# Linear attention with memory, and a Fourier mixing layer: a fourth part buffer, W8 in borrowed buffers, value weights loaded one per step, two chunks loaded earlier

## The chip, the core and the metric

The kernel runs on one core of a Trainium2 chip. The metric is the device time of one execution in microseconds. Before the change, three runs took 1090.06, 1090.17 and 1091.95 us, a median of 1090.17 us.

## The reference

Two independent results stand side by side in the output. The first is attention with a compressive memory over a sequence of 2048 positions, 576 channels and 32 heads of 18, cut into four segments of 512:

```python
q, k, v = x @ wq, x @ wk, x @ wv            # split into heads and 4 segments
for s in range(4):
    p = softmax(qs @ ks.T * scale + mask)   # causal inside the segment
    a_dot = p @ vs
    num, den = phi(qs) @ M, phi(qs) @ z + 1e-6   # phi(t) = t + 1 if t > 0 else exp(t)
    outs.append(g * num / den + (1 - g) * a_dot) # g = sigmoid(beta)
    M, z = M + phi(ks).T @ vs, z + phi(ks).sum()
a = concat(outs) @ wo
```

The second is a Fourier mixing layer with dense matrices on another input of the same shape:

```python
ar, ai = x @ dft_hid_re.T, x @ dft_hid_im.T
y = dft_seq_re @ ar - dft_seq_im @ ai
```

The output is `a` and `y` next to each other, 2048 by 1152.

## The kernel before

Every product is carried out on pairs of a high and a low part, so that the result keeps the precision of 32-bit floats: `split` (lines 53 to 55) lets ScalarE (ACT) copy the rounded high part and VectorE (DVE) subtract it from the raw values. The channel dimension, 576, is five row blocks of 128, where the fifth holds the last 64 channels twice, once for the high and once for the low part of the other operand.

The program has two stages. The first (lines 402 to 445) is the projection stage. It runs through the four segments. In each segment TensorE (PE) first opens the four query column blocks of the segment together (`open_qk`, line 196). Then `project_qk(s, m)` (line 208) finishes them and computes block 8, which holds the last 64 columns of both queries and keys (its weight is W8), and the key blocks 4 to 7. In segment 0 the order is 0 to 8. For each of the nine blocks, ACT and DVE cut the product, which stands in one of four rotating accumulators in PSUM, into three bfloat16 parts: ACT writes the first part into the part buffer `p` (line 219), DVE subtracts (`r`, line 220, which is the last reader of the accumulator in segment 0 and for keys), one step later ACT writes the second part (line 227) and GpSimd (POOL) the third (line 228), and one more step later a store sends `p` to `qd` or `kd` in device memory. Below, p(n) is the part buffer of the n-th block in the order of its segment, counted from 0, or the block m itself where the order is that of m, as in segment 0; in segments 1 to 3 the text names p(6) and p(7) by their key blocks 6 and 7. In segments 1 to 3 the query blocks also go through `phi` (line 172). Then, for each of four row blocks j, `project_v` (line 245) makes the values in two halves (`v`), `lookup` (line 303) reads the memory (`look`, `nd`, `am`, whose store to `amd` follows one step later), `k_natural` (line 237) transposes the keys back (`kt`, `knl`), and `accumulate` (line 278) adds to the memory on PE (line 286).

Deferred work goes through a clock of steps: `later(n, fn)` puts a call n steps ahead and `tick` (line 84) carries out what is due, so that the order on each engine is written out by hand. All loads and stores are issued by one queue, SyncE (SP), in program order; an instruction there that waits holds everything behind it.

The weights are loaded at the start. `load_w` (line 124) takes a buffer `raw` (five of them, `raw8` with four for W8) and issues the load at once; only the split waits for a step (lines 147 to 150). So the loads of the key weight, of W8 and of the value weight WV all stand on SP ahead of the first store. A warm-up of 32 small products (line 191) runs on PE before the first inputs have arrived. The part buffer `p` has three copies (line 217), `am` two (line 325).

In segment 3 the second stage is prepared: the Fourier weights are split (`h_split`, line 336), and the chunks of the other input are loaded (`c_load`, line 345, three buffers `craw`) and cut (`c_cut`, line 352). Chunks 0 to 2 are loaded there and chunks 0 and 1 cut on DVE; from then on `chunk(n)` (line 486) loads chunk n + 3 and cuts chunk n + 2 on POOL.

The second stage mixes the attention of 32 groups of heads with the Fourier products in one order on PE, which is fixed when the program is written (lines 749 to 756): `dense` gives its next product whenever its share of the estimated time is behind. The output projection closes the kernel.

Of the kernel before, what the change touches and what calls it, by code (L numbers as in the profile page):

```python
# [12 lines left out]
F32 = mybir.dt.float32  # L13
F32R = mybir.dt.float32r
F16 = mybir.dt.float16
BF16 = mybir.dt.bfloat16
# [6 lines left out]
S, D, H, DH, NSEG, L = 2048, 576, 32, 18, 4, 512  # L23
P = 128
# [12 lines left out]
def infini_attention_and_fnet(ctx: ExitStack, tc: tile.TileContext, xT, wqk, w8, wv, wo, beta, xtT, cT, hT, out):  # L37
    nc = tc.nc
    act, dve, pool, pe = nc.scalar, nc.vector, nc.gpsimd, nc.tensor
    dma = nc.sync.dma_start  # L40
# [12 lines left out]
    def split(hi, lo, raw, lo_engine=None):  # L53
        act.activation(hi, raw, AF.Copy)  # L54
        (lo_engine or dve).tensor_tensor(lo, raw, hi.bitcast(F32), OP.subtract)  # L55
# [25 lines left out]
    def later(n, fn, *a):  # L81
        due.setdefault(clock[0] + n, []).append((fn, a))
# [31 lines left out]
    def split_wk(w, k, raw):  # L114
        if k < 4:
            split(w[0][k], w[1][k], raw)
        else:
            t1, t2 = w[2], w[3]
            act.activation(t1, raw, AF.Copy)
            act.activation(t2, raw, AF.Copy)  # L120
            dve.tensor_tensor(t1[:64], raw[:64], t1[:64].bitcast(F32), OP.subtract)
            dve.tensor_tensor(t2[64:], raw[64:], t2[64:].bitcast(F32), OP.subtract)

    def load_w(src, cols, k, tag="raw"):
        raw = sb.tile([P, cols], F32, name=tag, tag=tag, bufs=5 if tag == "raw" else 4)
        dma(raw, src[k])
        return raw

    def weight(mk):
        return [[mk() for _ in range(4)] for _ in range(2)] + [mk() for _ in range(2)]  # L130

    def wide_tile(cols):
        return lambda: wide.tile([P, cols], F32R, name="wide", tag="wide")
# [9 lines left out]
        split_x(0, k)  # L143
        split_wk(WQ, k, raw)
    dma(g, bass.AP(tensor=beta.tensor, offset=beta.offset, ap=[[0, P], [1, H]]))
    WK, W8, WV = weight(wide_tile(L)), weight(lambda: sb.tile([P, P], F32R, name="w8", bufs=10)), weight(wide_tile(D))
    for w, src, cols, tag, when in ((WK, wqk[:, :, L:], L, "raw", (1, 1, 1, 1, 2)), (W8, w8, P, "raw8", (3, 3, 3, 4, 4)),
                                    (WV, wv, D, "raw", (5, 5, 6, 6, 7))):
        for k in range(5):
            later(when[k], split_wk, w, k, load_w(src, cols, k, tag))  # L150
    later(5, gates)

    pq_hi = sb.tile([P, 5, L], F32R, name="pq_hi")
# [36 lines left out]

    def warm_up():
        o = ps.tile([P, 1024], F32, name="kt", bufs=1)
        for _ in range(32):
            pe.matmul(o[:, :P], ident16, ident16, start=True, stop=True)

    def open_qk(s):
# [11 lines left out]
    def project_qk(s, m):  # L208
        if m in FIRST:
            o = FIRST.pop(m)  # L210
        else:
            o = ps.tile([P, L], F32, name="qk", tag="acc", bufs=4)
            chain(o, qk_terms(s, m))
        if m >= 4 and s < 3:
            KF[m] = sk.tile([P, L], F32, name="kf", bufs=5)
            act.activation(KF[m], o, AF.Copy)
        p = sb.tile([P, 3, L], BF16, name="p", bufs=3)
        r = sb.tile([P, L], F32, name="r", bufs=2)
        act.activation(p[:, 0], o, AF.Copy)
        dve.tensor_tensor(r, o, p[:, 0], OP.subtract)  # L220
        if s and (m < 4 or m == 8):
            n = P if m < 4 else 64
            c = m if m < 4 else 4
            phi(sb, "q", o[:n], n, pq_hi[:n, c], pq_lo[:n, c])

        def rest():
            act.activation(p[:, 1], r, AF.Copy)
            pool.tensor_tensor(p[:, 2], r, p[:, 1], OP.subtract)
            if m < 8:
                later(1, dma, (qd if m < 4 else kd)[s][(m % 4) * P:(m % 4 + 1) * P], p)  # L230
            else:
                later(1, dma, qd[s][4 * P:], p[:64])
                later(1, dma, kd[s][4 * P:], p[64:])

        later(1, rest)
# [67 lines left out]
    def lookup(s, j):  # L303
        js = slice(j * P, (j + 1) * P)
        nd = sb.tile([P, H, 19], F32, name="nd", bufs=2)
        o = []
        for c0, c1 in ((0, 3), (3, 5)):
            o.append(ps.tile([P, 3, 8, 19], F32, name="look", tag="acc", bufs=4))
            for c in range(c0, c1):
                for n, (a, m) in enumerate(((pq_hi, md_lo), (pq_hi, md_hi), (pq_lo, md_hi))):  # L310
                    pe.matmul(o[-1][:, c - c0], a[:, c, js], m[:, c], start=c == c0 and n == 0, stop=True,  # L311
                              skip_group_check=True)
            if c0 == 0:
                act.activation(nd[:, :21].rearrange("p (c h) e -> p c h e", c=3), o[0][:, :, :7], AF.Copy)
                yield
        act.activation(nd[:, 21:28], o[1][:, 0, :7], AF.Copy)
        act.activation(nd[:, 28:], o[1][:, 1, 4:], AF.Copy)
        dve.tensor_tensor(nd[:, 7:22:7], nd[:, 7:22:7], o[0][:, :, 7], OP.add)
        dve.tensor_tensor(nd[:, 28], nd[:, 28], o[1][:, 0, 7], OP.add)
        w = sb.tile([P, H, 1], F32, name="w", bufs=2)  # L320
        den = o[1][:, 2].rearrange("p h e -> p (h e)")[:, :H, None]
        dve.tensor_scalar(den, nd[:, :, DH:], 1e-6, None, op0=OP.add)
        dve.reciprocal(den, den)
        dve.tensor_tensor(w, den, g[:, :, None], OP.mult)
        am = sb.tile([P, H, DH], F32, name="am", bufs=2)
        pool.tensor_tensor(am, nd[:, :, :DH], w.to_broadcast([P, H, DH]), OP.mult)
        later(1, dma, amd[4 * s + j], am.rearrange("p h d -> p (h d)"))
        yield
# [7 lines left out]
    def h_split(ri, k):  # L336
        if k == 0:
            HW[ri] = weight(wide_tile(D))
        split_wk(HW[ri], k, HRAW.pop((ri, k)))

    c_raw, c_split = {}, {}
    CHUNKS = [c for ri in range(2) for c in
              [(xtT, tt, 5) for tt in range(NT)] + [(cT, (ri, tt, q), 4) for tt in range(NT) for q in range(4)]]

    def c_load(n):
        if n < len(CHUNKS):
            src, at, k = CHUNKS[n]
            t = sr.tile([P, 5, P], F32, name="craw", bufs=3)
            dma(t[:, :k], src[at])
            c_raw[n] = t  # L350

    def c_cut(n, engine=pool):
        if n < len(CHUNKS):
            raw = c_raw.pop(n)
            hi = sr.tile([P, 4, P], F32R, name="chi", bufs=3)
            lo = sr.tile([P, 4, P], F32R, name="clo", bufs=3)
            split(hi, lo, raw[:, :4], engine)
            t = None
            if CHUNKS[n][2] == 5:
                t = sr.tile([P, P], F32R, name="xtail", bufs=3)  # L360
                act.activation(t, raw[:, 4], AF.Copy)
                engine.tensor_tensor(t[64:], raw[64:, 4], t[64:].bitcast(F32), OP.subtract)
            c_split[n] = hi, lo, t
# [38 lines left out]
    for s in range(NSEG):  # L402
        more = s < 3
        if s == 0:
            warm_up()
        open_qk(s)
        if s:
            memory()
        else:
            tick()  # L410
        for n, m in enumerate((0, 1, 2, 3, 8, 4, 5, 6, 7) if s else range(9)):
            project_qk(s, m)
            tick()
            if not more and n >= 5:
                h_split(0, n - 5)
            if s in (1, 2) and n >= 4:
                load_x(s + 1, n - 4)
            if not more and n == 0:
                for k in range(5):
                    h_load(0, k)  # L420
            if not more and n == 4:
                p1k.close()
                sr = ctx.enter_context(tc.tile_pool(name="sb2r", bufs=1, side="right", reuse_waits="tile"))
                attention_tiles()
            if not more and n in (5, 6):
                stacks(sr, n - 5)
            if not more and n == 7:
                stack_load(0, 99)
                c_load(0)
        for j in range(4):  # L430
            if not more and j < 2:
                c_load(1 + j)
            project_v(s, j, lookup(s, j) if s else iter(()))
            if more:
                k_natural(j)
            tick()
            for k in ((0, 1), (2, 3), (4,), ())[j] if s == 0 else ():
                load_x(1, k)
            if more and j in (1, 2):
                split_x(s + 1, j - 1)  # L440
            if not more and j < 3:
                h_split(0, 4) if j == 0 else c_cut(j - 1, dve)
            if more and j:
                accumulate(j - 1)
    p1.close()
# [345 lines left out]
def _tail_twice(a):  # L791
    return np.concatenate([a, a[512:]], axis=0).reshape(5, P, a.shape[1])
# [26 lines left out]
```

## Time and profile before

| | us |
|---|---|
| median of three runs | 1090.17 |
| lowest and highest run | 1090.06, 1091.95 |
| the profiled execution | 1088.57 |
| its span in the profile | 1086.7 |
| segment 0 of the projections (start to the next `open_qk`) | 64.0 |
| segment 1 | 62.5 |
| segment 2 | 64.0 |
| segment 3 (to the first product of the second stage) | 60.4 |

The span is the time between the first and the last instruction that the profile shows; the execution's own time has 1.9 us around it. Times in the profile count from the start of the span. In its rows, "PE" is a product, "PEld" the loading of its stationary operand; an output and an input stand as `out<-in`, with the program's names. A row's bracket gives the idle time of the engine just before and what ended it.

### The profile page before, as it was taken

The numbers are of one execution on the slowest core, as the hardware profiler recorded it, in microseconds if no ns is written. First come the engines' busy times: TensorE is split into PE (matmuls) and PEld (weight loads), VectorE is DVE, ScalarE is ACT, GpSimd is POOL, SyncE is SP. The second block draws the span as 40 slices with busy tenths as digits, with TensorE's granted clock in tenths as the row PEclk, the third lists the DMA queues.
The fourth block names the chain that finished last, engine by engine and source line by source line (L and its number), as shares of the span: only waits on it lengthen the run. The fifth ranks groups of instructions, "written<-read, shape, count | busy, mean of one in ns | idle before, by whom it ended". The sixth has DMA issues, their size and how long they took to land.

```text
span 1086.7 us, 26387 instructions
## 1 busy us (share of the span) xinstructions
PE 1058.9 (97%) x9900; PEld 980.8 (90%) x9900; DVE 764.6 (70%) x1973; ACT 665.9 (61%) x1477; POOL 618.2 (57%) x716
## 2 busy tenths in 40 slices
PE   9898999989999999999999999999999999999998
PEld 7787989878999999999898999999999998999998
DVE  5544546565687877778888777887887888885343
ACT  5756566544576666666766666766666666666233
POOL 2455564644566666666575666656666666667000
PEclk9999999989999999999999999999999999999999
DMA  6425243356344454445443454335354455523474
GB/s 195 177 101 174 103 135 128 140 172 196 104 102 108 111 127 118 105 124 140 132 121 103 124 127 119 109 103 138 111 142 145 112 151 147 164 90 109 127 207 142
DMA packets 118480, 143.50 MB, mean 132 GB/s; under 512 B 45040, under 2 KB 77680, under 8 KB 118352
## 3 DMA queue, kind: packets, MB, share of 16 engines
q1 hardware_dynamic: 118352, 141.81, 45.1%
q8 instruction: 78, 1.28, 0.5%
q14 instruction: 50, 0.41, 0.1%
HBM read 102.32 MB, written 39.45 MB: 130 GB/s over the span
## 4 chain that ended last, share of the span: by engine, by line
PE 81%; DVE 7%; ACT 5%; DMA 3%; issue 2%; POOL 1%; SPq 1%; DVEq 0%; POOLq 0%; ACTq 0%
PE d L459 35%; PE s L618 6%; PE d L77 5%; PE v L77 4%; PE pv L686 4%; PE d L500 3%; PE d L501 3%; PE d L502 3%; PE t L653 3%; PE qk L204 3%; PE pv L687 2%; PE t L656 2%; PE m L286 2%; PE look L311 1%; PE qk L77 1%
## 5 line engine op out<-in xcount | busy, mean ns | idle before, releaser
L621 DVE CUSTOM_DVE_ANT_0 s<-s,causal 128x512 f32<-128x512 f32 (+3 forms) x512 | 249.6, 499 | 46.8 <-PE s L618 40.4
L55 POOL TENSOR_TENSOR clo<-craw,chi 128x512 fp32r<-128x512 f32 x158 | 209.9, 1328 | 113.8 <-ACT chi L54 92.2
L664 ACT ACTIVATE pf<-t 128x384 f32<-128x384 f32 (+1 forms) x384 | 203.1, 529 | 112.1 <-PE t L653 112.1
L459 PE MATMUL d<-wide,chi 128*128 128x288 f32 x1408 | 267.5, 307 | 0.0
L459 PEld LDWEIGHTS d<-wide,chi 128*128 128x128 f32 x1408 | 211.7, 189 | 5.0 <-issue 1.6
L459 PE MATMUL d<-wide,clo 128*128 128x288 f32 x704 | 181.3, 324 | 0.0
L663 ACT ACTIVATE phi<-t 128x384 f16<-128x384 f32 x256 | 124.9, 488 | 80.6 <-PE t L660 80.5
L675 DVE TENSOR_TENSOR plo<-pf,phi 128x512 f16<-128x512 f32 x128 | 136.1, 1063 | 31.3 <-ACT phi L672 30.5
L673 POOL TENSOR_TENSOR plo<-pf,phi 128x384 f16<-128x384 f32 x128 | 134.8, 1053 | 40.2 <-ACT pf L664 24.3
L618 PE MATMUL s<-ks,qs 108*128 108x512 bf16 (+3 forms) x512 | 131.9, 298 | 5.7 <-DVE negm L621 5.6
L459 PE MATMUL d<-ab,chi 128*128 128x288 f32 x640 | 127.1, 308 | 0.0
L459 PEld LDWEIGHTS d<-wide,clo 128*128 128x128 f32 x704 | 118.6, 189 | 5.1 <-issue 1.7
L667 POOL TENSOR_SCALAR_AFFINE_SELECT pf<-pf 128x512 f32<-128x512 f32 x128 | 86.4, 675 | 55.6 <-ACT pf L664 49.0
L54 ACT ACTIVATE chi<-craw 128x512 fp32r<-128x512 f32 x160 | 101.9, 637 | 16.3 <-DMA craw<-cT 6.8
L686 PE MATMUL pv<-vst,phi 128*128 128x55 bf16 x1280 | 104.0, 190 | 0.4 <-DVE og L706 0.3
L459 PEld LDWEIGHTS d<-ab,chi 128*128 128x128 f32 x640 | 98.3, 189 | 1.2
L687 PE MATMUL pv<-vst,plo 128*128 128x37 bf16 x1280 | 98.8, 180 | 0.0
L674 DVE TENSOR_TENSOR plo<-pf,phi 128x384 f16<-128x384 f32 x128 | 93.5, 731 | 2.0 <-ACT pf L664 2.0
L686 PEld LDWEIGHTS <-phi 128*128 128x128 f16 x1280 | 76.1, 96 | 19.0 <-DVE og L706 1.3
L459 PE MATMUL d<-ab,clo 128*128 128x288 f32 x320 | 85.5, 316 | 0.0
L500 PE MATMUL d<-wide,chi 128*128 128x288 f32 x256 | 85.1, 332 | 0.0
L672 ACT ACTIVATE phi<-pf 128x512 f16<-128x512 f32 x128 | 80.8, 632 | 0.9 <-POOL pf L667 0.7
(182 smaller groups left out, 2439.2 us busy)
## 6 DMA issues: line engine op xcount, KB each, us to landing
craw<-cT SPq DMA_DIRECT2D x128, 256.0 KB
qs<-qd SPq DMA_DIRECT2D x192, 72.0 KB
ks<-kd SPq DMA_DIRECT2D x192, 72.0 KB
craw<-xtT SPq DMA_DIRECT2D x32, 320.0 KB
out<-y SPq DMA_DIRECT2D x31, 288.0 KB
vd<-vs SPq DMA_DIRECT2D x16, 440.0 KB
vst<-vd SPq DMA_DIRECT2D x32, 220.0 KB
qd<-p SPq DMA_DIRECT2D x16, 384.0 KB
```

The lines of the kernel that those rows point to most:

```text
L55: (lo_engine or dve).tensor_tensor(lo, raw, hi.bitcast(F32), OP.subtract)
L77: pe.matmul(o, a, b, start=n == 0, stop=n == len(terms) - 1)
L459: pe.matmul(o[h], a, b[:, h * 288:h * 288 + 288], start=start, stop=stop)
L500: pe.matmul(o, xh[:, k], wl[k][:, cs], start=k == 0, stop=False)
L618: pe.matmul(o[:, c:c + w], q[:, i * P:w], k[:, :w], start=True, stop=True)
L621: dve.tensor_tensor_reduce(o[:, c:c + w], o[:, c:c + w], CAUSAL[0][:, L - w:], scale=-1.0, scalar=-LOWEST, op0=OP.add, op1=OP.min, accum_o ...
L663: act.activation(hi[:, r:r + w], o[:, :w], AF.Exp, bias=LIFT, scale=SCALE)
L664: act.activation(f[:, r:r + w], o[:, :w], AF.Exp, bias=LIFT, scale=SCALE)
L673: pool.tensor_tensor(lo[:, 896:], f[:, 896:], hi[:, 896:], OP.subtract)
L675: dve.tensor_tensor(lo[:, :512], f[:, :512], hi[:, :512], OP.subtract)
L686: pe.matmul(o, hi[:, c:c + P], v, start=j == 0, stop=False)
L687: pe.matmul(o[:, 18:], lo[:, c:c + P], v[:, 18:], start=False, stop=j == i)
```

## The change

- The part buffer `p` has four copies, `am` one.
- W8 is stored with the five row blocks side by side, so that it comes in two loads (four blocks of 128 columns together, and the fifth) instead of five. They land in the two `qe` buffers, which `phi` uses from segment 1 on. Four row blocks are split by one operation of 512 columns each on ACT and DVE, at step 4.
- The value weights are no longer loaded ahead: block k is loaded at step 3 + k and split three steps later, in steps 6 to 10 instead of 5 to 7.
- The warm-up has 44 products instead of 32.
- In segment 3, chunks 3 and 4 are loaded right after chunks 0 and 1 have been cut, and `c_load` skips them later.

```diff
-    WK, W8, WV = weight(wide_tile(L)), weight(lambda: sb.tile([P, P], F32R, name="w8", bufs=10)), weight(wide_tile(D))
-    for w, src, cols, tag, when in ((WK, wqk[:, :, L:], L, "raw", (1, 1, 1, 1, 2)), (W8, w8, P, "raw8", (3, 3, 3, 4, 4)),
-                                    (WV, wv, D, "raw", (5, 5, 6, 6, 7))):
-        for k in range(5):
-            later(when[k], split_wk, w, k, load_w(src, cols, k, tag))
+    WK, WV = weight(wide_tile(L)), weight(wide_tile(D))
+    for k in range(5):
+        later((1, 1, 1, 1, 2)[k], split_wk, WK, k, load_w(wqk[:, :, L:], L, k))
+    w8_hi, w8_lo = (sb.tile([P, 4, P], F32R, name=f"w8{n}") for n in "hl")
+    W8 = [[w[:, k] for k in range(4)] for w in (w8_hi, w8_lo)] + [sb.tile([P, P], F32R, name=f"w8t{n}") for n in "ab"]
+    raw8 = [sb.tile([P, L], F32, name="qe", bufs=2) for _ in range(2)]
+    dma(raw8[0], w8[:, :L])
+    dma(raw8[1][:, :P], w8[:, L:])
+
+    def split_w8():
+        split(w8_hi, w8_lo, raw8[0].rearrange("p (k c) -> p k c", k=4))
+        split_wk(W8, 4, raw8[1][:, :P])
+
+    later(4, split_w8)
+
+    def load_wv(k):
+        later(3, split_wk, WV, k, load_w(wv, D, k))
+
+    for k in range(5):
+        later(3 + k, load_wv, k)
...
-        for _ in range(32):
+        for _ in range(44):
...
-        p = sb.tile([P, 3, L], BF16, name="p", bufs=3)
+        p = sb.tile([P, 3, L], BF16, name="p", bufs=4)
...
-        am = sb.tile([P, H, DH], F32, name="am", bufs=2)
+        am = sb.tile([P, H, DH], F32, name="am", bufs=1)
...
-        if n < len(CHUNKS):
+        if n < len(CHUNKS) and n not in c_seen:
+            c_seen.add(n)
...
                 h_split(0, 4) if j == 0 else c_cut(j - 1, dve)
+            if not more and j in (1, 2):
+                c_load(2 + j)
```

More of the change, by code (lines that the diff above doesn't have):

```diff
@@ L122, in split_wk, with load_w @@
             dve.tensor_tensor(t2[64:], raw[64:], t2[64:].bitcast(F32), OP.subtract)
-    def load_w(src, cols, k, tag="raw"):
-        raw = sb.tile([P, cols], F32, name=tag, tag=tag, bufs=5 if tag == "raw" else 4)
+    def load_w(src, cols, k):
+        raw = sb.tile([P, cols], F32, name="raw", tag="raw", bufs=5)
         dma(raw, src[k])
@@ L339, in h_split @@
         split_wk(HW[ri], k, HRAW.pop((ri, k)))
-    c_raw, c_split = {}, {}
+    c_raw, c_split, c_seen = {}, {}, set()
     CHUNKS = [c for ri in range(2) for c in
@@ L800 @@
         "wqk": _tail_twice(np.concatenate([wq[:, :512], wk[:, :512]], axis=1)),
-        "w8": _tail_twice(np.concatenate([wq[:, 512:], wk[:, 512:]], axis=1)),
+        "w8": _tail_twice(np.concatenate([wq[:, 512:], wk[:, 512:]], axis=1)).transpose(1, 0, 2).reshape(P, 5 * P),
         "wv": _tail_twice(wv),
```

## The prediction

> **What bounds the kernel now.** I read the page first, then the windows by stage, the waits, the chain of waits, and the timelines of single engines around each gap. Stage borders are the starts of the next projection (`open_qk`) on PE.
>
> ```profile
> PE 1058.9 (97%) x9900; PEld 980.8 (90%) x9900; DVE 764.6 (70%) x1973; ACT 665.9 (61%) x1477; POOL 618.2 (57%) x716
> ```
>
> PE is busy 1058.9 of 1086.7 us, so 27.8 us of gaps plus what half clock costs is all that a change of buffers can win. The windows show where it is:
>
> ```profile
> 0.00:64.02 64.02, 58.19 (x336) 51.19 (x337) 37.01 (x66) 41.59 (x84) 23.05 (x31) 0.97 0.54 180
> 64.02:126.50 62.48, 59.16 (x379) 53.61 (x379) 31.57 (x70) 39.08 (x84) 35.93 (x36) 1.00 0.37 129
> 126.50:190.47 63.97, 60.57 (x380) 55.05 (x379) 33.07 (x70) 38.79 (x83) 37.25 (x37) 0.97 0.35 123
> 190.47:250.86 60.39, 54.98 (x314) 49.53 (x313) 36.29 (x59) 32.28 (x66) 35.01 (x38) 0.94 0.45 157
> 300.00:1010.00 710.00, 705.36 (x7561) 653.77 (x7561) 565.09 (x1550) 464.87 (x1038) 461.03 (x539) 1.00 0.45 122
> ```
>
> After the length comes PE's busy time; the third number from the end is the granted clock. The four projection segments hold 18 us of gaps and lose more at clock 0.94 to 0.97; the 710 us after 300 hold under 5. In the waits, three lines belong to the change:
>
> ```profile
> ACT p L219 <- DMA qd<-p: 6.6, 1, 6.6
> ACT p L219 <- DMA kd<-p: 5.6, 4, 1.5
> ACT chi L54 <- DMA craw<-xtT: 5.4, 1, 5.4
> ```
>
> Line 219 writes a part buffer `p`; it waits for the store of the `p` three steps earlier. The same stores stand in the chain:
>
> ```profile
> 24.22 6.46 DMA qd<-p
> 94.67 5.53 DMA kd<-p
> 157.17 5.57 DMA kd<-p
> 256.34 4.67 DMA craw<-xtT
> ```
>
> And this is what PE pays (in brackets: idle before, and who ended it), with two rows of line 121 and the start:
>
> ```profile
> 5.67 0.80 PE L204 MATMUL qk<-xh,wide 128*128 128x512 f32 x1 [0.65 <-ACT wide L54]
> 32.24 0.50 PE L77 MATMUL qk<-xh,wide 128*128 128x512 f32 x1 [2.42 <-DVE r L220]
> 101.73 0.34 PE L311 MATMUL look<-mdl,pq_hi 128*128 128x152 f32 x1 [1.91 <-DVE r L220]
> 164.27 0.34 PE L311 MATMUL look<-mdl,pq_hi 128*128 128x152 f32 x1 [1.95 <-DVE r L220]
> 263.69 0.38 PE L618 MATMUL s<-ks,qs 108*128 108x512 bf16 x1 [2.05 <-DVE negm L621]
> 38.12 0.74 DVE L121 TENSOR_TENSOR wide<-raw,wide 64x576 fp32r<-64x576 f32 x1
> 233.55 1.66 DVE L121 TENSOR_TENSOR wide<-raw,wide 64x576 fp32r<-64x576 f32 x1 [0.24 <-ACT wide L119]
> ```
>
> PE waits for `r` (line 220) because `r` frees the accumulator, `r` waits for `p`, and `p` for the store.
>
> **Segment 0: part buffers, W8, value weights.** Before, SP issues five W8 loads and then five value-weight loads ahead of the first store; the fifth W8 load waits 3.3 us for its raw buffer. So the store of p(0), ready on POOL at 21.24, is issued at 24.22 and lands at 30.68; p(3) needs its buffer and starts at 30.79. After, W8 is two loads that wait for no split (the `qe` buffers are idle in segment 0), each value-weight load stands between two stores, and p(3) has a fourth buffer. p(4) is the first that waits, for a store now issued near 21.3. I bound its landing by 2.9 us (192 KB at 93.36, waited for until 96.24) and 6.5 us (row above, beside five loads): 24.2 to 27.8. ACT reaches p(4) near 25.9; I take no wait, and for the upper bound 0.8 us on PE, since ACT's step is 2.43 us (p at 41.89 and 44.32) against PE's 3.18 (14 matmuls of 0.227) and makes most of 1.9 us good by the ninth part.
> Removed: the 2.42 us gap, and the half clock behind it: the 14 matmuls from 32.24 end at 37.15, 4.91 us against 3.18, so 1.73. With ACT no longer late, the gap before the second `kt` goes (48.34 to 49.67, 1.33), and the next 15 line-286 matmuls take 1.51 instead of 1.99 (0.48). Together 5.96.
> Added: the fifth value weight is split at the tick right before `project_v(0, 0)`. The same order stands in the trace for an earlier part: `kf` starts on ACT at 36.35, then `p`, lines 119 and 120; DVE does `r`, 121, 122 and ends at 39.64: 3.3 us after `kf`, which starts when the last projection ends. PE reaches the last tail matmul after 13 of 0.134, 1.74 us. So 1.6 us of new wait; queued behind it on PE are all of v, `kt` and accumulate. If POOL runs beside the two subtractions they cost 1.66 and 1.70 (the row at 233.55 and its successor) instead of 0.74 and 0.75, so 3.5 at most; POOL's next operation comes after both have begun, so I take 1.6. The Trainium skill ("SBUF — State Buffer", Who interferes with whom) calls this an exclusive lock that the first comer keeps; the two rows agree, and by it the wait is 1.6 or 3.5 and little between.
> On SP each value-weight load now stands behind a store that waits for POOL. The last follows the store of p(3) (POOL until about 26.8), is issued near 27.3, lands by 33.8 at 6.5 us, and is split at 37: 3 us of cover. W8's splits are one of 512 columns instead of four of 128 on ACT and DVE, done by about 24, 9 us before PE needs them: nothing. Net of the segment: -4.3.
>
> **Warm-up, 32 to 44 matmuls.** 32 took 3.60 us from 1.43; then 0.65 idle; from 5.67 PE runs at a pitch of 0.43 us until 8.9, then 0.23. Twelve more (0.11 each, 1.35) close the gap and end at 6.38 if cold. At worst the clock rises no sooner than before and 0.7 is lost; at best it rises before 6, and then the query weight's tail (DVE until 15.33) limits the gain to about 1.2. The Trainium skill ("TensorE: Matmul & The Clock Gate", Part 1) has a free-running busy window of 3.4 us; with no gap it rises between 4.8 and 8.3 by that, a gain of 0.2 to 1.2. From the rows alone: 3.2 us of gapless work (5.67 to 8.9) sufficed, and work is now gapless from 1.43, which speaks for the better end, but one execution shows one phase: I take -0.7.
>
> **Segments 1 and 2.** p(6) waits 1.24 and p(7) 1.50 us (gaps on ACT at 96.24 and 100.28), and 1.29 and 1.55 in segment 2. With four buffers p(6) needs the store issued by 89.5 (5.6 us: 95.1, wanted at 95.0) and p(7) the one at 93.4, landed by 96.2, wanted at 97.4. `r(7)` then ends at 98.86, and PE arrives from v at 98.9: it is next, so the whole ACT saving counts, -2.8 each. Segment 2 also runs the v product at 166.49 in 3.50 instead of 1.88 us, half clock after gaps of 1.95 and 0.76; without the first I count that off, -1.6.
>
> **Segment 3** has no `p` wait on ACT; its gaps (2.44, 0.99, 1.98) come from DVE's weight splits and memsets ahead of `r`. Zero. Fourth and fifth chunk: now issued when DVE has freed a raw buffer (243.7 and 249.2), not at 256.34 behind the last value stores; landing by 4.67, chi(3) finds its data and the 2.05 gap goes. Next late would be chi(5): its load still waits for POOL's cut (256.94), lands by 261.7 and is wanted at 264.2 (266.27 less 2.05); between 264 and 300 PE has no gap. The value stores queued behind the two loads are ready later (244.9, 250.3), so they lose nothing. -2.05.
>
> **One `am` buffer.** `am` now waits for its predecessor's store: issued 107.21, next `am` 111.74, 4.5 us; between the landings of 2.9 and 5.6, at most 1.1 late. Behind it on POOL is `knl` (done 115.1), which PE wants near 118.5. Zero; the cover is 3.4 us.
>
> **Sum.** 4.3 + 0.7 + 2.8 + 2.8 + 1.6 + 2.05 = 14.25. The profiled execution took 1088.57 (span 1086.7 and 1.9 around it), so 1074.3; it lies 1.6 below the median 1090.17, which becomes 1075.9.
>
> **Rivals.** (1) The new v wait is long enough, or falls so, that the clock drops: gaps of 1.95 and 0.76 did it in segment 2, 1.91 and 0.76 did not in segment 1. Costs 1.7, and with no warm-up gain leaves 11.9: 1078.3. Chance 0.15.
> (2) Another landing binds: if the store by 89.5 takes 7.2 (the first input's row in the chain, 2.67 to 9.86), p(6) waits again and the gain of segments 1 and 2 is gone: 7.2 less, 1083.1. Against: 5.6 is the longest store in those segments. 0.08.
> (3) Slower: the single `am` buffer. If its store lands later than 4.5 + 3.4 = 7.9 us, `knl` holds `accumulate`, six times in segments 1 and 2 at 1 us per us; beyond 10.3 us all of 14.25 is spent, and at 10.6 the kernel is 2 us slower, 1092. No row is above 7.2: 0.03, and 0.01 for what I do not see.
> (4) The waits are only renamed (the stores land at the rate the DMA engines grant, and the fourth buffer shifts the wait): no change, 1090. Against: DMA share 0.35 in segment 2. 0.02.
> The forecast keeps 0.71. About 0.2%, 2.2 us, is what a measurement of this kernel can tell from no change. The range goes from full warm-up gain and no half clock in segment 3 (2.5 us from 231.91 on: 1072.9), less the 1.9 by which the three runs differ (1071.0), to rival 1 with the upper bounds of p(4) and of the subtractions (1.9 + 0.8: 1081.0), widened by 1 towards rival 2.
>
> **What would show it.** Right: no `p` wait in segments 0 to 2, a gap of 1.6 us in the first v product, ended by the fifth value weight's split, no wait on craw at the fourth chunk, segments 1 and 2 near 59.6 us. Wrong: p(4) waiting past 28, a 2 us gap before the first `look` pair's end, `am` on the chain, or the gaps moving behind 300.

## The result, and the profile after

The changed kernel takes 1076.7 us (median of four runs, 1076.37 to 1077.89); the kernel before took 1090.12 us beside it (four runs, 1089.61 to 1091.95). The ratio is 0.9876, with a 95% interval of 0.9859 to 0.9893: 13.4 us faster. The profiled execution took 1077.89 us (span 1076.2), the longest of its four runs.

The page's line of engines:

```profile
PE 1058.4 (98%) x9912; PEld 981.6 (91%) x9912; DVE 763.4 (71%) x1970; ACT 665.7 (62%) x1474; POOL 617.2 (57%) x716
```

PE's busy time is almost what it was (1058.9) although it runs twelve products more; the span is 10.5 us shorter, so gaps went. The windows by stage (length, PE's busy time, then the other engines; third from the end the granted clock) show which:

```profile
0.00:63.91 63.91, 59.40 (x348) 52.80 (x349) 36.08 (x63) 41.70 (x81) 22.41 (x31) 0.95 0.57 185
63.91:123.43 59.52, 58.76 (x380) 53.53 (x379) 31.67 (x70) 38.85 (x84) 35.91 (x36) 1.00 0.37 131
123.43:182.92 59.49, 58.73 (x379) 53.54 (x379) 33.08 (x70) 38.47 (x83) 37.24 (x37) 1.00 0.37 133
182.92:242.18 59.26, 55.73 (x315) 50.45 (x314) 36.31 (x59) 31.93 (x66) 34.56 (x38) 0.91 0.50 166
300.00:1010.00 710.00, 705.00 (x7532) 653.93 (x7531) 560.17 (x1536) 460.00 (x1025) 454.23 (x532) 1.00 0.45 122
```

Segments 1 and 2 now take the same 59.5 us at full clock. Segment 0 has gained 0.1 us in this execution, segment 3 1.1. The 710 us after 300 hold 5.0 us of gaps, as before (4.6). In the waits, no line has `p` waiting for a store; of the chunk's wait 0.3 us is left. ACT now stands longer for a load of the key weight: the first line here is from the waits of the kernel before, the other two are from the changed kernel.

```profile
ACT wide L119 <- DMA raw<-wqk: 0.6, 1, 0.6
ACT wide L119 <- DMA raw<-wqk: 2.7, 1, 2.7
ACT chi L54 <- DMA craw<-xtT: 0.3, 1, 0.3
```

The stores of `p` are gone from the chain of waits. In the projection stage, two loads stand there alone (start, duration): the fifth block of the query weight and the fifth block of the key weight, both slices of `wqk`.

```profile
5.26 7.87 DMA raw<-wqk
15.39 4.39 DMA raw<-wqk
```

What PE still waits for there, from its timeline (in brackets the idle time before, and what ended it):

```profile
37.84 0.53 PE L77 MATMUL v<-wide,xh 128*128 128x288 f32 x2 [0.94 <-DVE wide L55]
40.26 0.61 PE L77 MATMUL v<-wide,xt 128*128 128x288 f32 x1 [1.76 <-DVE wide L121]
41.05 0.61 PE L77 MATMUL v<-wide,xt 128*128 128x288 f32 x1 [0.18 <-DVE wide L122]
...
100.87 0.50 PE L77 MATMUL v<-wide,xh 128*128 128x288 f32 x2 [0.76 <-DVE vr L278]
...
218.36 0.85 PE L77 MATMUL v<-wide,xh 128*128 128x288 f32 x2 [2.45 <-DVE r L235]
224.36 0.85 PE L77 MATMUL v<-wide,xh 128*128 128x288 f32 x2 [1.08 <-DVE vr L278]
```

The gap at the fourth product of segment 0 and those before the second `look` are gone. The first v product of segment 0 has a new wait, 0.94 + 1.76 + 0.18 = 2.9 us (called the v wait below), and PE runs at half clock from about 40.2 to 47.0 (in the window from 34 to 48 the granted clock is 0.76). PE arrived at that product at 35.56 instead of 40.32, so 4.8 us were won there and nearly all lost again. The start of this wait stands on ACT and DVE:

```profile
37.69 0.58 ACT L231 ACTIVATE kf<-qk 128x512 f32<-128x512 f32 x1
...
38.65 0.68 ACT L119 ACTIVATE wide<-raw 128x576 fp32r<-128x576 f32 x1
39.22 0.68 ACT L120 ACTIVATE wide<-raw 128x576 fp32r<-128x576 f32 x1
```

```profile
39.47 0.74 DVE L121 TENSOR_TENSOR wide<-raw,wide 64x576 fp32r<-64x576 f32 x1
40.24 0.76 DVE L122 TENSOR_TENSOR wide<-raw,wide 64x576 fp32r<-64x576 f32 x1
```

From `kf` to the end of the second subtraction it is 3.3 us, as the prediction took from the kernel before. But `kf` does not start when the last projection product ends (about 35.8): ACT is 1.9 us late.

### The profile page after: what moved, and what is told of

It reads as the page before. It is cut to its first block, busy times and chain, and to the rows that moved or that the text cites. A ratio compares the mean times of both kernels' runs of the same rounds, so it can differ in the third digit from the quotient of the medians.

```text
span 1076.2 us, 26389 instructions
## 1 busy us (share of the span) xinstructions
PE 1058.4 (98%) x9912; PEld 981.6 (91%) x9912; DVE 763.4 (71%) x1970; ACT 665.7 (62%) x1474; POOL 617.2 (57%) x716
## 4 chain that ended last, share of the span: by engine, by line
PE 84%; DVE 7%; ACT 5%; issue 2%; DMA 2%; SPq 1%; POOL 0%; DVEq 0%; POOLq 0%; ACTq 0%
PE d L477 35%; PE s L636 6%; PE d L77 6%; PE v L77 5%; PE pv L704 4%; PE d L518 3%; PE d L519 3%; PE d L520 3%; PE qk L77 3%; PE t L671 3%; PE qk L219 3%; PE pv L705 2%; PE t L674 2%; PE m L301 2%; DVE r L235 1%
```

## The experiments

Each ratio is to the kernel before on the same chip; a thousandth is 1.09 us. "Segment" times run from the first query product of one segment to that of the next.

**The changed kernel again, twice.**

> The changed kernel once more, for a second profiled execution. In the first, segment 0 took 63.9 us instead of the 59 of the prediction: the first v product waited 2.9 us for the value weights (0.94, 1.76 and 0.18), and PE ran at half clock from 40.3 to about 47, at a cost of 3.4. Theory A (the wait is fixed by the order, the half clock is a matter of where the wait falls): again 2.5 to 3.3 us of waits in that product, with or without half clock, segment 0 60.5 or 64, time 1076 to 1078. Rival (the slow segment 0 was one odd execution): waits of 1.6 us or less, segment 0 near 59.

> The changed kernel as it is, beside the three others of this call on one chip: 0.987 to 0.988 of the kernel before, and a wait of 2 to 3 us in the first v product as in its two earlier profiles, whichever way the half clock falls.

Measured: 1074.76 us (ratio 0.9876, 0.9859 to 0.9893), and 1076.51 us (0.9875, 0.9854 to 0.9896). The three profiles, with the kernel before and the prediction's terms:

| us | before | predicted change | first | again | third |
|---|---|---|---|---|---|
| segment 0, from the start | 63.85 | -5.0 (4.3 + 0.7) | 63.75 | 60.83 | 63.00 |
| segment 1 | 62.49 | -2.8 | 59.51 | 59.53 | 59.52 |
| segment 2 | 63.97 | -4.4 | 59.50 | 59.47 | 59.52 |
| segment 3 to the first s product | 60.55 | 0 | 59.42 | 59.23 | 59.35 |
| the rest of the span | 835.84 | -2.05 | 834.02 | 833.84 | 834.01 |
| span | 1086.7 | -14.25 | 1076.2 | 1072.9 | 1075.4 |

Segments 1 to 3 and the rest repeat within 0.2 us. Segment 0 varies by 2.9. Its v wait is 2.9, 2.1 and 2.9 us; the second lies below the 2.5 to 3.3 of theory A, and so does its time below 1076 to 1078, but it is not the 1.6 of the rival. From the first v product to the next segment it takes 28.2, 25.8 and 28.1 us, where a version without wait and half clock (below) takes 21.6. So 28.2 - 21.6 - 2.9 = 3.7 us in the first, 2.1 and 3.6 in the others, are half clock and what else a wait costs PE. Two versions that wait 1.05 and 1.44 us at full clock (below) leave 0.5 us by the same reckoning, so half clock itself costs about 3.2, 1.6 and 3.1 us. This agrees with its length: a granted clock of 0.76, 0.88 and 0.76 from 34 to 48 is 6.7, 3.4 and 6.7 us at half, and half of each is lost.

**Three part buffers again.**

```diff
-        p = sb.tile([P, 3, L], BF16, name="p", bufs=4)
+        p = sb.tile([P, 3, L], BF16, name="p", bufs=3)
```

> Three part buffers again, the rest as changed. Theory A (the fourth buffer takes away the waits of segments 1 and 2): the two gaps on ACT before the seventh and eighth part come back in segments 1 and 2 (2.8 us each), segments 1 and 2 near 62.4 or 64, and segment 0 loses up to 2 more at the fourth part; 7 to 9 us slower than the changed kernel, 1084 to 1086. Rival (the waits are only renamed, the gain of segments 1 and 2 came from elsewhere): within 1 us of the changed kernel, 1076 to 1078.

Measured: 1083.84 us, ratio 0.9953 (0.9935 to 0.9971), 9.1 us above the changed kernel beside it. The waits and then the chain of waits of this kernel have the stores of `p` back:

```profile
ACT p L234 <- DMA kd<-p: 5.5, 4, 1.5
```

```profile
92.61 5.49 DMA kd<-p
156.63 5.59 DMA kd<-p
```

Before the second `look`, PE waits 1.89 us at 99.63 and 1.92 at 163.75, the gaps of the kernel before. Segments 1 and 2 need the fourth buffer. Segment 0 does not: it takes 61.8 us here, PE has no gap at the fourth product, and ACT waits 0.3 us for a store there. The loss of up to 2 us at the fourth part that theory A gave is not there.

**Four part buffers alone, on the kernel before** (one `am` buffer makes room).

```diff
-        p = sb.tile([P, 3, L], BF16, name="p", bufs=3)
+        p = sb.tile([P, 3, L], BF16, name="p", bufs=4)
-        am = sb.tile([P, H, DH], F32, name="am", bufs=2)
+        am = sb.tile([P, H, DH], F32, name="am", bufs=1)
```

> The kernel before with four part buffers (and a single am buffer to make room), nothing else of the change. Theory A (the stores of p set the waits of segments 0 to 2): segment 0 keeps five W8 loads ahead of the first store, but p(3) no longer needs that store, so the 2.42 us gap at the fourth product shrinks or goes; segments 1 and 2 lose their ACT waits, 2.8 each, and the half clock behind the 1.95 us gap of segment 2 goes with them: 7 to 11 us below the kernel before. Rival (the fourth buffer only renames the wait; the gain came from the order of the loads): less than 3 us below it.

Measured: 1078.14 us, ratio 0.9891 (0.9865 to 0.9918): 12.0 us below the kernel before, more than theory A gave. By segments 3.56, 2.96, 4.48 and 1.15 us, 12.15 up to the first s product. So the buffer alone does nearly all of it. (In this profile 1.2 of the 3.56 us in segment 0 are the start: the query tail products begin at 18.90 instead of 20.13, which the buffer does not reach; and 2.1 of the 12.15 us are lost again behind the first s product, where half clock now falls behind the late chunk's gap: 0.76 from 250 to 257 us.) ACT still waits for the store in segment 0, and PE hardly does (waits; then PE's timeline, where the fourth product had waited 2.42):

```profile
ACT p L219 <- DMA qd<-p: 3.1, 1, 3.1
```

```profile
32.06 0.50 PE L77 MATMUL qk<-xh,w 128*128 128x512 f32 x1 [0.30 <-DVE r L220]
```

**All of the change but W8 and the value weights** (the kernel before with four part buffers, one `am` buffer, 44 warm-up products and the early chunk loads).

> Everything of the change except its W8 and value-weight part: the kernel before with four part buffers, 44 warm-up matmuls, early chunk loads and one am buffer. Theory A (the prediction's segment 0: the store order of the changed loads is needed, and costs a v wait of 1.6): about 3 to 4 us above the changed kernel, since the store of p(0) stays behind the loads. Rival B, from the run with four part buffers alone (its v product starts at 35.40 without a wait): four buffers have already taken the gap of segment 0, and the value-weight order only adds its wait: equal to the changed kernel or up to 3 us below it, 1073 to 1076 where the changed kernel has 1075 to 1077.

Measured: 1075.05 us, ratio 0.9866 (0.9844 to 0.9888), beside 0.9875 for the changed kernel on the same chip. Rival B holds: on balance the W8 and value-weight part brings nothing that can be measured. ACT's timeline, then PE's:

```profile
31.32 0.60 ACT L219 ACTIVATE p<-qk 128x512 bf16<-128x512 f32 x1 [3.68 <-DMA qd<-p]
```

```profile
32.77 0.50 PE L77 MATMUL qk<-xh,w 128*128 128x512 f32 x1 [0.69 <-DVE r L220]
...
41.62 0.33 PE L242 MATMUL kt<-ident,kf 128*128 128x128 f32 x1 [1.01 <-ACT kf L216]
46.82 0.65 PE L241 MATMUL kt<-ident,kf 128*128 128x128 f32 x4 [1.16 <-DVE ke L176]
```

With five loads ahead of the first store, p(4) waits 3.68 us for it, yet a wait that falls one step later than before costs PE 0.69 there instead of 2.42. PE then stands 1.01 and 1.16 us at `kt`, for ACT's `kf` and for `ke`, and 0.18 behind it: gaps that the kernel with the moved loads does not have. There is no v wait and no half clock in this segment 0: from the v product to the next segment it takes 24.9 us, and it ends at 61.00, against 60.83 to 63.75 with the loads moved.

**The value weights one step earlier.**

```diff
-        later(3 + k, load_wv, k)
+        later(2 + k, load_wv, k)
```

> Value weights loaded and split one step earlier (step 2 + k, split at 5 + k), the rest as changed. Theory A (the fifth value weight, split in the last step, holds the first v product, and the half clock comes from that hole): no wait for the splits of value weights, no half clock in segment 0, segment 0 near 58 us; 3 to 6 us faster than the changed kernel, 1071 to 1074. Rival (ACT is the bound there, the wait moves to another part of its queue): the same 2 to 3 us of gaps on PE before or in the v product, ended by line 235, less than 1 us gained.

Measured: 1071.28 us, ratio 0.9842 (0.9823 to 0.986), 3.5 us below the changed kernel beside it. The v wait does not go; PE's timeline:

```profile
37.50 0.40 PE L77 MATMUL v<-wide,xt 128*128 128x288 f32 x1 [0.66 <-DVE wide L121]
38.29 0.40 PE L77 MATMUL v<-wide,xt 128*128 128x288 f32 x1 [0.39 <-DVE wide L122]
```

But 1.05 us of wait brings no half clock in this execution (the granted clock from 34 to 48 is 1.00), and that is the larger part: the segment ends 2.5 us earlier than in the changed kernel beside it, with 1.0 of it from the wait.

**W8 loaded behind the first store.**

```diff
-    dma(raw8[0], w8[:, :L])
-    dma(raw8[1][:, :P], w8[:, L:])
+    def load_w8():
+        dma(raw8[0], w8[:, :L])
+        dma(raw8[1][:, :P], w8[:, L:])
...
-    later(4, split_w8)
+    later(4, load_w8)
+    later(7, split_w8)
```

> W8 loaded behind the first store (step 4) and split at step 7, the rest as changed. Theory A (the 256 KB load of W8, issued right behind the key weight's fifth block, slows that block: 4.4 us to its landing instead of 2.8, and ACT, in order, is late by 1.6 from there on): the key weight's fifth block lands near 18.2 again, the value weights are split 1.5 us earlier and the wait in the first v product falls to 1.6 or less; 1 to 4 us faster than the changed kernel. Rival (that landing differs from run to run, W8 has no part in it): landing and wait as in the changed kernel, less than 0.5 us of difference.

Measured: 1074.5 us, ratio 0.9873 (0.9852 to 0.9894), the same as the changed kernel. The key weight's fifth load took 3.46 us here, inside the 2.60 to 4.39 of the changed kernel's three profiles, and the v wait was 1.76 + 0.39 us. Theory A asked for 2.8 us and 1.6 or less, so nothing here shows that W8's load delays the key weight's.

**Three steps of segment 0 moved**: value weights earlier, the key weight's last split behind p of the next step, the gates later.

```diff
-        later((1, 1, 1, 1, 2)[k], split_wk, WK, k, load_w(wqk[:, :, L:], L, k))
+        later((1, 1, 1, 1, 3)[k], split_wk, WK, k, load_w(wqk[:, :, L:], L, k))
...
-        later(3 + k, load_wv, k)
+        later(2 + k, load_wv, k)
-    later(5, gates)
+    later(12, gates)
```

> The changed kernel with three steps of segment 0 moved: value weights one step earlier, the fifth split of the key weight one step later (behind p of the next step, so that ACT does not stand waiting for its load), the gates at step 12 instead of 5. Theory A (ACT's lateness behind the key weight's fifth load sets the end of segment 0, not the value weights' order): the wait in the first v product goes altogether, 1 to 2 us below the run with the value weights one step earlier, some 5 us below the changed kernel (ratio to the kernel before 0.983 or less). Rival (what is left is ACT's own step time): the same as with the value weights one step earlier, ratio 0.984 to 0.985.

Measured: 1070.48 us (1070.16 to 1070.9), ratio 0.9823 (0.9797 to 0.9848), 2.1 us below the step before by the ratios, and 5.8 below the changed kernel; the intervals of the two versions overlap, so the trace has to say it. In its chain of waits segment 0 is nothing but PE:

```profile
1.43 4.79 PE kt L209 x44
6.22 12.82 PE qk L219 x56
19.04 15.87 PE qk L77 x70
34.90 3.70 PE v L77 x28
```

The v wait has gone altogether, and the next segment starts at 56.4. ACT no longer stands for the key weight's load, and `kf` of the last block starts 0.1 us behind the last projection product. Theory A holds: what set the end of segment 0 was ACT, which stood 2.7 us for that load in the changed kernel and then went on at 2.43 us a step. Three steps were moved at once; the value weights alone left 1.05 us of the v wait (above), and what the key weight's split and the gates each add to that was not run apart.

**32 warm-up products.**

```diff
-        for _ in range(44):
+        for _ in range(32):
```

> The changed kernel with 32 instead of 44 warm-up matmuls. Theory A (the twelve more raise the clock earlier and all of it reaches the end): 0.7 us above the changed kernel, 0.2 to 1.2. Rival (the first v product waits for weights that ACT and DVE finish at their own time, so what PE wins at the start it waits there): no difference, under 0.2 us.

Measured: 1074.23 us, ratio 0.9856 (0.983 to 0.9882): not slower than the changed kernel's 0.9875 and 0.9876. The expected 0.7 us is not seen, and an effect of that size stays open in the times. Its profile, which is the fastest of its six runs (1070.88 us), shows one reason. The chain of waits:

```profile
5.69 13.30 PE qk L219 x56
18.99 15.88 PE qk L77 x70
```

PE was at full clock almost from its first product here, with only 32. By the start of the query tail products in PE's timeline (0.16 us ahead of the chain's piece), the four profiles with 32 have 20.13 (the kernel before), 20.69, 18.90 and 18.83 us, the ten with 44 18.88 to 19.42. Two of the four with 32 start slowly, none of the ten with 44: the twelve more remove the slow start, 0.5 us in the mean (19.64 against 19.14). This profile also has the segment 0 that was forecast: ACT stands 0.6 us for the key weight's fifth load, the v wait is 1.05 + 0.39 us, the granted clock from 34 to 48 is 1.00, and the segment takes 58.3 us.

**The early chunk loads alone, on the kernel before.**

```diff
     def c_load(n):
-        if n < len(CHUNKS):
+        if n < len(CHUNKS) and n not in c_seen:
+            c_seen.add(n)
...
+            if not more and j in (1, 2):
+                c_load(2 + j)
```

> The kernel before with the fourth and fifth chunk of the raw input loaded in segment 3, nothing else. Theory A: the gap of 2.05 us at the fourth chunk goes and nothing takes its place: 2 us below the kernel before. Rival (the next landing or weight split ends at the same time): less than 0.5 us below it.

Measured: 1087.04 us, ratio 0.9976 (0.9959 to 0.9994), 2.6 us below the kernel before, between 0.7 and 4.5. PE has no gap between 240 and 280 us, where the kernel before had one of 2.05. From the first s product to the end its trace is 1.2 us shorter (834.6 against 835.8). Theory A holds, though neither the times nor the trace fix its 2 us.

**Segment 3: weight splits set ahead of the deferred copies.** This is about the gaps that the change had left.

```diff
             project_qk(s, m)
-            tick()
             if not more and n >= 5:
                 h_split(0, n - 5)
+            tick()
```

> The changed kernel with the four weight splits of segment 3 set ahead of the deferred copies, so that DVE takes r before the split and not behind it. Theory A (the gaps of segment 3, 2.4 and 1.0 and 2.0 us, are r standing behind L55 and a memset): they shrink by at least 3 us in sum, 3 to 5 us below the changed kernel. Rival (the split and p then meet on ACT instead, or the weights come late for the attention): under 1 us.

Measured: 1072.68 us, ratio 0.9845 (0.9821 to 0.987), 3.8 us below the changed kernel on the same chip. DVE's timeline in this kernel, and then in the changed one:

```profile
207.87 0.69 DVE L235 TENSOR_TENSOR r<-qk,p 128x512 f32<-128x512 f32 x1
208.47 1.51 DVE L55 TENSOR_TENSOR wide<-raw,wide 128x576 fp32r<-128x576 f32 x1
210.24 0.91 DVE L386 MEMSET ks<- 32x1024 f32 x1 [0.25 <-issue]
211.18 0.69 DVE L235 TENSOR_TENSOR r<-qk,p 128x512 f32<-128x512 f32 x1
```

```profile
208.76 0.69 DVE L235 TENSOR_TENSOR r<-qk,p 128x512 f32<-128x512 f32 x1
210.73 1.28 DVE L55 TENSOR_TENSOR wide<-raw,wide 128x576 fp32r<-128x576 f32 x1 [1.27 <-ACT wide L54]
212.26 0.91 DVE L386 MEMSET ks<- 32x1024 f32 x1 [0.25 <-issue]
213.20 0.69 DVE L235 TENSOR_TENSOR r<-qk,p 128x512 f32<-128x512 f32 x1
```

From one `r` to the next it is 3.3 us instead of 4.4, since DVE no longer waits 1.27 us for the split's high part between them. The time came as expected, but not as gaps: PE's gaps in segment 3 sum to 2.8 us (0.34, 0.32, 2.14) where they were 3.5 in the changed kernel beside it (2.45, 1.09). What is shorter is the run of `r` steps: from the start of the segment to the last `r` it is 33.8 us (181.86 to 215.68) instead of 38.0 (182.04 to 220.03), and behind it both take 21.4. In the changed kernel half clock on PE filled part of the longer time (0.83 from 212 us to the end of the segment, 1.00 here). The segment takes 55.2 us instead of 59.4.

**Both together, a version that beats both kernels.**

> The three moved steps of segment 0 and the moved weight splits of segment 3 together. Theory A: both gains add, 0.978 to 0.980 of the kernel before, 1066 to 1068. Rival (segment 3 is bound by ACT as much as by DVE): as without the moved splits, 0.982 to 0.983.

Measured: 1068.42 us (1067.45 to 1070.76), ratio 0.9809 (0.9783 to 0.9834): 8.1 us below the changed kernel on the same chip, 21.6 below the kernel before. The median is just above theory A's 1066 to 1068. A gap of 2.72 us at 226.18, in front of a v product and ended by `vr`, is left in segment 3.

## Why the prediction was right, and where its steps were not

**The mechanism of segments 1 and 2** was right in kind and size: -2.8 and -4.4 foretold, -3.0 and -4.5 measured, and the kernel with three buffers shows the other side. The half clock of segment 2 went with its first gap.

**Segment 0** is the step that failed, in two places. The first is the term "1.6 us of new wait". It rests on `kf`, "which starts when the last projection ends", so on an ACT that is not late by then. In the first profile `kf` of the last block starts 1.9 us late: the key weight's fifth load, which took 2.77 us in the profile of before, took 4.39, ACT stood 2.7 us for it, and at 2.43 us a step it did not make that good. For the same reason the first store went out at 22.93 and not near 21.3. The two subtractions took 0.74 and 0.76 us, so POOL did not lengthen them, as the prediction had it. Seven profiles split the key and value weights at the steps of the changed kernel (four of them with something else changed), and in them the v wait grows with the time that ACT stands for this load, with small exceptions near the top:

| profile | ACT stands | v wait | granted clock, 34 to 48 | segment 0 |
|---|---|---|---|---|
| 32 warm-up products | 0.64 | 1.44 | 1.00 | 58.3 |
| changed kernel, again | 1.10 | 2.09 | 0.88 | 60.8 |
| W8 behind the first store | 1.78 | 2.15 | 0.88 | 61.1 |
| segment 3's splits moved | 2.09 | 2.75 | 0.76 | 62.9 |
| three part buffers | 2.10 | 2.94 | 0.88 | 61.8 |
| changed kernel, third | 2.18 | 2.87 | 0.76 | 63.0 |
| changed kernel, first | 2.67 | 2.88 | 0.76 | 63.8 |

Where ACT stands as briefly as in the kernel before (0.6), the wait is about the 1.6 of the forecast and the segment near its 59 us. So the mechanism was right, and its size hung on a load time that one profile did not bound; why the load takes longer in some executions stays open.

The second place is rival 1, the clock that drops behind the new wait. It came true in six of these seven profiles, where its chance was put at 0.15, and at about 1.6 us in one and 3.2 in two of the changed kernel's, where it was priced 1.7: the price is that of 3.4 us at half clock, and two of the three have twice that. The net of segment 0 with its warm-up was -0.1 to -3.0 us, not -5.0.

The attribution failed too. The 2.42 us gap was put down to the loads and the buffer together, and either of them takes it away: four buffers alone leave 0.30 us of it, and the moved loads with three buffers leave none. The W8 and value-weight part did take away ACT's wait for the store (3.7 us without it) and, as foretold, the gaps at `kt` (1.01, 1.16 and 0.18 without it), but it put the v wait and half clock in their place, and on balance the kernel without it is as fast as the whole change.

**Warm-up** at -0.7 fits the traces (0.5 in the mean of starts, of four and ten profiles) and can't be seen in the times. **The chunks** at -2.05 measured -1.8 to -2.0 in the traces of the changed kernel, with nothing late next at the fifth; alone it showed -1.2. **Segment 3** at zero was low by 1.1 to 1.3. Up to its last `r` it takes 38.0 us in the kernel before and in every version that keeps its order, whatever PE's gaps and clock are there, so DVE's `r` steps set that part; with the splits moved it is 33.8. What got shorter is the part behind, 22.6 us before and 21.2 to 21.4 in the three profiles. The cause of that is open: the kernel with four buffers alone has 21.4 there, but the one with three buffers again has 20.6. **One `am` buffer** at nothing: no wait for its store appears in the waits.

**The sum** said 1074.3 for a profiled execution; the three took 1077.89, 1074.62 and 1077.1. That the median of 1075.9 came so close to 1076.7 is in part luck: segment 3, put at nothing, gave back 1.2 of the 2.0 to 4.9 us that segment 0 fell short. Adding 1.6 for the low profile of before was right, and the changed kernel's first profile lies 1.2 above its own median. Rivals 2 to 4 did not occur.

## What to carry to other kernels

When a gap comes from a store that a buffer waits for, try the one more buffer alone first: here it was worth 12.0 us where the whole change was worth 13.4, and the reordering of loads that came with it lost by a wait of its own what it won, until three more steps were moved. When PE arrives earlier at a place, ask which other engine is the latest there by its own timeline, including its waits for loads, whose durations in one profile are no bound. Price a wait on PE of two microseconds or more at about double, since the clock behind it can halve: in segment 0 it did so behind all six v waits of 2.1 to 2.9 us, and behind neither of the two of 1.05 and 1.44.

## What the runs showed of the hardware

Half clock comes without a long idle time. It followed gaps of 0.94, 1.76 and 0.18 us within 4.2 us (clock 0.76 from 34 to 48), and of 1.70 and 0.39 in another execution, but not of 0.66 and 0.39, nor of 1.05 and 0.39. The size of the gaps alone does not decide: gaps of 1.00, 1.17 and 0.18 us at and behind `kt` in segment 0 of the kernel with the early chunk loads alone had half clock behind them (0.64 from 52 to 56 us), and gaps of 1.01, 1.16 and 0.18 at the same products of the kernel without the W8 and value-weight part had none (1.00). The Trainium skill ("TensorE: Matmul & The Clock Gate", Part 1) has the clock return to half after an idle window of about 3.4 us; here no single gap reached 3.4 us, so the measurement decides that less is enough.

Half clock came in stretches of one length. In all fourteen profiles every stretch in the projection stage lasts 3.4 us, or two or three times that; in the three of the changed kernel the one in segment 0 goes from 40.2 to 47.0, from 40.2 to 43.7 and from 39.3 to 46.1.

The same load of a weight block (128 x 512 floats, the fifth of the key weight) took 2.60, 3.91 and 4.39 us in three executions of one kernel, issued at 15.2 to 15.4 us in all of them. No run here shows why.
